# Mish written back into its PSUM bank, and both halves of the result taken from there

## The chip, the core and the metric

One core of a Trainium2 chip runs the whole program, which is launched once. The metric is the device time in microseconds (us): the median over the runs of a kernel. TensorE is called PE in the profile, VectorE DVE, ScalarE ACT and GpSimd POOL.

## The reference

Block-causal attention over four batches of 576 tokens with eight heads of width 64, then an MLP with Mish, then RMS norm and a gated MLP. Only the first MLP is touched by the change.

```
x = attention(q, k, v)                  # 2304 tokens x 512
h = x @ w_in                            # 2304 x 2048
g = h * tanh(log1p(exp(h)))             # Mish
y = g @ w_out                           # 2304 x 512
xn = y / rms(y) * rms_g
out = (silu(xn @ w_gate) * (xn @ w_val)) @ w_out2
```

## The kernel before

**Numbers.** A float32 operand of a product is scaled and split into two float16 halves, "high" and "low" (the rest after the high half). A product is then three passes of float16 matmuls, high by high, high by low and low by high. So each result that goes into another product has to be turned into two halves first: one instruction rounds it to the high half, a second subtracts that from the value and rounds the rest to the low half.

**The first MLP.** Tokens are taken in nine tiles of 256 (t), and d_ff in eight steps (s) of two blocks of 128. A step of `mlp1_h` fills one PSUM bank `ph` (tag `h`, a ring of two banks) with 24 matmuls of 128x256, in two groups of 12: 128 partitions by 512 float32. Then, in every tile but the first, which is computed in float32 and has no halves, three instructions follow:

- line 1410, ACT: Mish of the bank with a scale per partition, written to an SBUF tile `f` (a ring of two),
- line 1419 (DVE), 1422 (ACT) or 524 (POOL): the high half `g[:, 0]`, from `f` with a scale per partition; the three engines are alternatives,
- line 1427, DVE: the low half `g[:, 1]` from `f`, the scale and the high half.

This is done 64 times (eight steps in each of eight tiles). `mlp1_y` then takes `g` (tag `g16`, a ring of four) as the weights of 12 matmuls of 128x512 into two PSUM banks `y`.

**What goes on beside it.** The attention of later tokens is interleaved with it. For each head, PE makes the scores `s` (lines 989, 1000 and 1007, a ring of two banks), DVE takes the row maximum `mx` (1024), DVE or POOL makes a bias of it (1033), ACT makes the exponential `e` (1049), and `e` is split into halves `p`: high by DVE, ACT or POOL (1123, 1126, 524), low by POOL or DVE (1130). A DMA transposes `p` into `pt`, and PE multiplies it with v (1161, `x`). Mish and the exponential need different ACT tables, so ACT loads a table whenever it goes from one to the other (`ACT_TABLE_LOAD` under lines 1049 and 1410). The weights of the second MLP are loaded and split in the same stretch, too.

**The order of the work.** The program records its operations with their reads, writes and alternatives, and a planner (`Plan`) computes from costs and a key of each operation in what order every engine issues, and on which engine an operation with alternatives runs. What comes out is a fixed order for each engine. The keys are shifted by two tables, `SHIFT` (by part of the work) and `FINE` (by number of the operation). A buffer's ring is a wait: the first writer of a buffer waits for all users of the buffer that had its place before. In the second MLP, the accumulators reuse the rings `g16` and `f` (`acc_of`).

Of the kernel before, what the change touches and what calls it, by code (L numbers as in the profile page):

```python
# [334 lines left out]
def block_attention_mish_mlp_gated_mlp(  # L335
# [13 lines left out]
    nc = tc.nc  # L349
# [599 lines left out]
    def attention(b, i, at, pace):  # L949
# [20 lines left out]
        def scores(keys, at):  # L970
# [43 lines left out]
            es = [buf("at", [P, NTT * P], F32, f"e{b}_{i}_{h}", "e", 3) for h in keys]  # L1014
# [27 lines left out]
            for y, (h, e) in enumerate(zip(keys, es)):  # L1042
                if n % P:
                    op(POOL, 125, lambda e=e: nc.gpsimd.memset(e()[:, n : kt * P], 0.0), w=[(e, "pad")], at=at)
                for z, (c0, w) in enumerate(parts):
                    acc = (ssum, h) if len(parts) == 1 else (sump, 2 * key + z)
                    op(
                        ACT, t_act(w, 2, True, True),
                        lambda y=y, z=z, c0=c0, w=w, acc=acc, e=e, h=h: nc.scalar.activation(  # L1049
                            out=e()[:, c0 : c0 + w], in_=ts[z]()[:, y, :], func=AF.Exp, bias=bias()[:, h : h + 1],  # L1050
                            scale=c_op(), accum_out=acc[0]()[:, acc[1] : acc[1] + 1],
                        ),
                        r=[(ts[z], y), (bias, h)] + c_in, w=[(e, z), acc], at=at, table="exp",
                    )
# [211 lines left out]
        for gi, keys in enumerate(groups):  # L1266
            a = at + pace * gi / len(groups)
            plan.part = f"a{b}_{i}_{(4 if b == 0 else 2) * gi // len(groups)}"
            es = scores(keys, a)
            pv, pt = probs(keys, es, a)  # L1270
# [76 lines left out]
    def mlp1_h(t, s):  # L1347
# [49 lines left out]
        if whole:  # L1397
            if n < G_START:
                g32 = plan.part_of(spares, n)
            else:  # L1400
# [7 lines left out]
        e = buf("m1", [P, W], F32, f"f{n}", "f", F_BUFS)  # L1408
        op(
            ACT, t_act(W, 1, True), lambda: nc.scalar.activation(out=e(), in_=phf(), func=AF.Mish, scale=cs()),  # L1410
            r=[ph, (ch[t], q0)], w=[e], at=at, table="mish",
# [4 lines left out]
        hv = lambda: e().rearrange("p (g t) -> p g t", g=SC)  # L1416
        sc = lambda: ich[t]()[:, q0 : q0 + 1]
        op(
            DVE, t_dve2(W, 1), lambda: nc.vector.tensor_scalar_mul(g16()[:, 0], hv(), sc()), r=[e, (ich[t], q0)],
            w=[(g16, 0)], at=at,  # L1420
            alts=[(ACT, t_act(W, 1),
                   lambda: nc.scalar.activation(out=g16()[:, 0], in_=hv(), func=AF.Copy, scale=sc())),  # L1422
                  (POOL, t_pool1(W, 1), lambda: pool_copy(g16()[:, 0], hv(), sc()))],
        )
        op(
            DVE, t_dvett(W, 1),
# [3 lines left out]
            r=[e, (ich[t], q0), (g16, 0)], w=[(g16, 1)], at=at,  # L1430
# [869 lines left out]
```

## Time and profile before

| | |
|---|---|
| median of 3 runs | 951.97 us (951.47 to 953.11) |
| the profiled execution | 951.73 us |
| its span, first to last instruction | 949.9 us |
| granted TensorE clock, mean | 0.999 |
| PE, DVE, ACT, POOL busy | 921.5, 807.5, 657.5, 550.8 us |

The profiled execution lies 0.24 us under the median, and its time is 1.8 us above its span. The stretch of the 64 steps goes from 137 to 560 us. Busy time of PE is the union of the recorded spans of its matmuls; in the first 60 us it has filler matmuls in it, too (`shared<-idle_in`).

### The profile page before, as it was taken

Reading aid. Unit: us, or ns where it says so; the run is one execution under the profiler, and the core shown is the slowest. Engines: PE = TensorE matmul, PEld = TensorE weight load, DVE = VectorE, ACT = ScalarE, POOL = GpSimd, SP = SyncE. Lnnn points to the kernel's source line nnn. Section 1 sums busy time; section 2 is a strip of 40 time slices with the busy share of each in tenths; the row PEclk is TensorE's granted clock in tenths of the full one; section 3 lists DMA queues with packets and bytes.
Section 4 is the critical chain, followed back from the end, with each engine's and each line's share of the span. In section 5 each row is a group of like instructions: output and inputs, shape, how many; then the busy total and the mean of one; then the engine's idle time right before and its main releaser. Section 6 shows DMA issues by size and latency. Waiting matters only on the chain. (4 is left out here: it accounts for less than half of the span.)

```text
span 949.9 us, 20061 instructions
## 1 busy us (share of the span) xinstructions
PE 921.5 (97%) x7241; PEld 632.4 (67%) x7241; DVE 807.5 (85%) x1837; ACT 657.5 (69%) x1369; POOL 550.8 (58%) x688
## 2 busy tenths in 40 slices
PE   9999999998999999999999999999999999999997
PEld 7785457566577757757576745767676666767675
DVE  5899988997886777889877978989999999997666
ACT  4659679999799878889786546657665665553541
POOL 2348245774474654577754839568857697562322
PEclk9999999999999999999999999999999999999999
DMA  9764596779877796778985557826384560708011
GB/s 231 220 198 127 180 179 124 128 133 181 142 132 133 115 167 112 166 129 179 185 174 87 114 167 136 176 58 131 91 180 78 129 128 24 128 8 164 14 67 68
DMA packets 317187, 125.45 MB, mean 132 GB/s; under 512 B 296352, under 2 KB 296352, under 8 KB 317088
## 3 DMA queue, kind: packets, MB, share of 16 engines
q1 hardware_dynamic: 317088, 124.17, 62.4%
q8 instruction: 57, 0.93, 0.4%
q14 instruction: 42, 0.34, 0.1%
HBM read 50.07 MB, written 12.98 MB: 66 GB/s over the span
## 5 line engine op out<-in xcount | busy, mean ns | idle before, releaser
L1384 PE MATMUL h<-x,w1i 128*128 128x256 f16 x1536 | 180.2, 273 | 1.5 <-ACT f L1410 0.8
L1445 PE MATMUL y<-w1o,g 128*128 128x512 f16 x768 | 177.5, 379 | 2.2 <-DVE g L1427 1.1
L1384 PEld LDWEIGHTS <-w1i 128*128 128x128 f16 x1536 | 146.9, 98 | 24.0 <-issue 1.6
L1989 PE MATMUL o<-w2o,pp 128*128 128x256 f16 x1134 | 138.6, 273 | 2.2 <-DVE pp L1899 1.2
L1989 PEld LDWEIGHTS <-pp 128*128 128x128 f16 x1134 | 110.5, 98 | 26.3 <-issue 3.2
L1445 PEld LDWEIGHTS <-g 128*128 128x128 f16 x768 | 71.2, 98 | 79.7 <-issue 2.2
L1830 PEld LDWEIGHTS <-w2g 128*128 128x128 f16 x756 | 73.8, 98 | 47.9 <-issue 3.2
L1830 PEld LDWEIGHTS <-w2v 128*128 128x128 f16 x756 | 73.9, 98 | 44.9 <-issue 0.9
L1024 DVE TENSOR_REDUCE mx<-s 128x1 f32<-128x512 f32 (+4 forms) x128 | 70.3, 556 | 22.3 <-PE s L990 19.8
L1049 ACT ACTIVATE e<-s,bias,cS 128x512 f32<-128x512 f32 (+4 forms) x120 | 72.5, 607 | 14.3 <-POOL bias L1033 6.2
L1830 PE MATMUL v_u<-xnT,w2v 128*128 128x384 f16 x432 | 81.5, 326 | 0.3 <-DVE wc L659 0.2
L1830 PE MATMUL g_u<-xnT,w2g 128*128 128x384 f16 x432 | 78.9, 326 | 0.3
L1130 POOL TENSOR_TENSOR p<-e,p 128x384 f16<-128x384 f32 (+4 forms) x61 | 58.5, 960 | 18.2 <-DVE p L1123 6.8
L1427 DVE SCALAR_TENSOR_TENSOR g<-f,ich,g 128x512 f16<-128x512 f32 x64 | 57.9, 910 | 8.9 <-ACT g L1422 6.3
L1161 PEld LDWEIGHTS <-pt 128*128 128x128 f16 x1128 | 48.1, 98 | 22.6 <-DMA pt<-p 8.4
L1830 PE MATMUL v<-xnT,w2v 128*128 128x384 f16 x324 | 61.5, 326 | 0.0
L1830 PE MATMUL g<-xnT,w2g 128*128 128x384 f16 x324 | 61.1, 326 | 0.2
L1161 PE MATMUL x<-v,pt 128*128 128x64 f16 (+1 forms) x1128 | 55.0, 199 | 4.8 <-DMA pt<-p 4.7
L1049 ACT ACT_TABLE_LOAD x39 | 50.0, 1283 | 3.5 <-DVE bias L1033 2.9
L1410 ACT ACT_TABLE_LOAD x39 | 50.0, 1283 | 1.7 <-DVE g L1427 0.9
L1410 ACT ACTIVATE f<-h,ch 128x512 f32<-128x512 f32 x64 | 43.4, 685 | 8.0 <-PE h L1384 5.1
L1130 DVE TENSOR_TENSOR p<-e,p 128x512 f16<-128x512 f32 (+4 forms) x51 | 39.3, 773 | 4.1 <-ACT p L1126 2.5
(343 smaller groups left out, 2121.8 us busy)
## 6 DMA issues: line engine op xcount, KB each, us to landing
wir<-in_moe_w_in_dram SPq DMA_DIRECT2D x16, 512.0 KB, 5.5
wor<-in_moe_w_out_dram SPq DMA_DIRECT2D x16, 512.0 KB, 4.2
w2rg<-in_moe_w_gate_dram SPq DMA_DIRECT2D x24, 256.0 KB, 3.2
w2rv<-in_moe_w_val_dram SPq DMA_DIRECT2D x24, 256.0 KB, 3.5
w2ro<-in_moe_w_out_dram SPq DMA_DIRECT2D x24, 256.0 KB, 2.7
q<-in_q_dram SPq DMA_DIRECT2D x16, 256.0 KB, 3.9
k<-in_k_dram SPq DMA_DIRECT2D x16, 256.0 KB, 3.9
v<-in_v_dram SPq DMA_DIRECT2D x15, 256.0 KB, 4.0
```

The lines of the kernel that those rows point to most:

```text
L1024: lambda z=z, cols=cols: nc.vector.reduce_max(out=mx()[:, cols], in_=ts[z](), axis=AX.X),
L1049: lambda y=y, z=z, c0=c0, w=w, acc=acc, e=e, h=h: nc.scalar.activation(out=e()[:, c0 : c0 + w], in_=ts[z]()[:, y, :], func=AF.Exp, bias=bi ...
L1130: lo = lambda eng, z=z, ev=ev: eng.tensor_tensor(out=view(p16)[:, z, :, 1, :], in0=ev(0, kt), in1=view(p16)[:, z, :, 0, :], op=ALU.subtract)
L1161: nc.tensor.matmul(xt()[:, cols, :], pv(z)[:, t, ph, :], v16[b, t]()[:, vh, key * w : key * w + w], start=(t == 0 and y == 0), stop=(t == ...
L1384: nc.tensor.matmul(ph()[:, g, :], w1i[fq]()[:, cc, wh, f * P : (f + 1) * P], x()[:, xh * NCC + cc, :], start=(z == 0), stop=(z == 3 * NCC ...
L1410: ACT, t_act(W, 1, True), lambda: nc.scalar.activation(out=e(), in_=phf(), func=AF.Mish, scale=cs()),
L1427: lambda: nc.vector.scalar_tensor_tensor(out=g16()[:, 1], in0=hv(), scalar=sc(), in1=g16()[:, 0], op0=ALU.mult, op1=ALU.subtract),
L1445: nc.tensor.matmul(yps[t, m](), g16()[:, gh, g, m * P : (m + 1) * P], w1o[f]()[:, wh, :], start=(f == 0 and z == 0), stop=(f == NF1 - 1 an ...
L1830: nc.tensor.matmul(b(), w[wo]()[:, wh, cc, :], x()[:, (2 * xo + xh) * 2 + cc, :], start=(first and i == 0), stop=(i == 5), skip_group_chec ...
L1989: nc.tensor.matmul(b()[:, side, :], pps[r][po]()[:, gh, m * P : (m + 1) * P], w[wo]()[:, wh, r, :], start=(first and i == 0), stop=(i == 5 ...
```

## The change

- Mish (line 1410) is written back into `ph`, in place, not into `f`. The ring `f` is gone (`F_BUFS` 2 to 0).
- The high half is taken from `ph`. Its engine is ACT, with DVE as the alternative; POOL is no alternative any more.
- The low half is taken by DVE from `ph` and the high half. So the bank is in use until the low half is done.
- The ring `g16` has six buffers, not four (`G_BUFS`); the two take the place of the two of `f`, of the same size. The six accumulators that reused `g16` and `f` in the second MLP now reuse the six of `g16`.
- `SHIFT` and `FINE` are replaced by other tables, so the order of the whole program is another, the attention and the second MLP included. The count of the recorded operations is the same.
- The ring of `e` keeps its three buffers and gets a name, `E_BUFS`.

```diff
-        e = buf("m1", [P, W], F32, f"f{n}", "f", F_BUFS)
         op(
-            ACT, t_act(W, 1, True), lambda: nc.scalar.activation(out=e(), in_=phf(), func=AF.Mish, scale=cs()),
-            r=[ph, (ch[t], q0)], w=[e], at=at, table="mish",
+            ACT, t_act(W, 1, True), lambda: nc.scalar.activation(out=phf(), in_=phf(), func=AF.Mish, scale=cs()),
+            r=[ph, (ch[t], q0)], w=[ph], at=at, table="mish",
         )
         table_ops.append(plan.ops[-1])
 
         g16 = buf("m1", [P, 2, SC, T1], F16, f"g{n}", "g16", G_BUFS)
-        hv = lambda: e().rearrange("p (g t) -> p g t", g=SC)
+        hv = lambda: ph()
         sc = lambda: ich[t]()[:, q0 : q0 + 1]
         op(
-            DVE, t_dve2(W, 1), lambda: nc.vector.tensor_scalar_mul(g16()[:, 0], hv(), sc()), r=[e, (ich[t], q0)],
+            ACT, t_act(W, 1, True),
+            lambda: nc.scalar.activation(out=g16()[:, 0], in_=hv(), func=AF.Copy, scale=sc()), r=[ph, (ich[t], q0)],
             w=[(g16, 0)], at=at,
-            alts=[(ACT, t_act(W, 1),
-                   lambda: nc.scalar.activation(out=g16()[:, 0], in_=hv(), func=AF.Copy, scale=sc())),
-                  (POOL, t_pool1(W, 1), lambda: pool_copy(g16()[:, 0], hv(), sc()))],
+            alts=[(DVE, t_dve(W, 1), lambda: nc.vector.tensor_scalar_mul(g16()[:, 0], hv(), sc()))],
         )
         op(
-            DVE, t_dvett(W, 1),
+            DVE, t_dve(W, 1),
             lambda: nc.vector.scalar_tensor_tensor(
                 out=g16()[:, 1], in0=hv(), scalar=sc(), in1=g16()[:, 0], op0=ALU.mult, op1=ALU.subtract
             ),
-            r=[e, (ich[t], q0), (g16, 0)], w=[(g16, 1)], at=at,
+            r=[ph, (ich[t], q0), (g16, 0)], w=[(g16, 1)], at=at,
         )
...
-X_BUFS, F_BUFS, G_START, G_BUFS = 2, 2, 4, 4
+X_BUFS, F_BUFS, G_START, G_BUFS = 2, 0, 4, 6
...
+E_BUFS = 3
```

## Rows read from the trace of the kernel before

**Rows 1.** The page's first part: busy time, share of the span, instructions.

```profile
PE 921.5 (97%) x7241; PEld 632.4 (67%) x7241; DVE 807.5 (85%) x1837; ACT 657.5 (69%) x1369; POOL 550.8 (58%) x688
```

**Rows 2.** Windows: stretch, its length, busy time of each engine (instructions), clock, DMA.

```profile
0.00:137.00 137.00, 132.12 (x931) 91.03 (x932) 114.51 (x279) 93.81 (x237) 57.24 (x81) 1.00 0.70 188
137.00:560.00 423.00, 406.42 (x3620) 279.02 (x3621) 355.12 (x933) 348.42 (x690) 257.12 (x374) 1.00 0.76 145
560.00:950.00 390.00, 382.99 (x2692) 262.38 (x2690) 337.83 (x627) 215.30 (x442) 236.41 (x234) 1.00 0.46 99
```

**Rows 3.** Windows inside the stretch of the 64 steps.

```profile
core 0: us, PE busy (x) PEld busy (x) DVE busy (x) ACT busy (x) POOL busy (x), PEclk, DMA share, GB/s
137.00:160.00 23.00, 21.51 (x210) 17.18 (x211) 20.13 (x61) 19.78 (x39) 11.42 (x19) 1.00 0.71 138
160.00:200.00 40.00, 36.35 (x319) 23.32 (x318) 38.62 (x104) 39.25 (x95) 30.96 (x46) 1.00 0.76 131
200.00:250.00 50.00, 44.91 (x425) 30.12 (x423) 42.41 (x130) 45.93 (x79) 29.09 (x42) 1.00 0.87 157
250.00:300.00 50.00, 48.51 (x443) 34.84 (x440) 40.17 (x96) 43.73 (x96) 29.72 (x47) 1.00 0.84 149
300.00:350.00 50.00, 49.22 (x445) 34.03 (x443) 33.97 (x85) 41.82 (x81) 26.68 (x41) 1.00 0.75 125
350.00:400.00 50.00, 48.99 (x461) 33.43 (x459) 40.56 (x142) 40.16 (x69) 25.00 (x37) 1.00 0.73 140
400.00:450.00 50.00, 47.48 (x466) 34.79 (x464) 44.56 (x107) 44.13 (x98) 37.37 (x64) 1.00 0.83 150
450.00:500.00 50.00, 49.46 (x469) 31.94 (x466) 40.81 (x96) 39.01 (x72) 31.98 (x41) 1.00 0.87 183
500.00:560.00 60.00, 60.00 (x410) 39.36 (x409) 53.88 (x117) 34.61 (x71) 34.89 (x41) 1.00 0.55 127
```

**Rows 4.** Waits of PE from 137 to 560: total us, times, longest.

```profile
PE s L989 <- ACT e L1049: 5.6, 9, 1.4
PE x L1161 <- DMA pt<-p: 4.7, 9, 1.0
...
PE h L1384 <- ACT f L1410: 0.8, 3, 0.4
```

**Rows 5.** Groups by line: shapes, count, busy us, mean ns, idle before.

```profile
L1427 DVE SCALAR_TENSOR_TENSOR g<-f,ich,g 128x512 f16<-128x512 f32 x64 | 57.9, 910 | 8.9 <-ACT g L1422 6.3 <-POOL g L524 2.1
L1410 ACT ACT_TABLE_LOAD x39 | 50.0, 1283 | 1.7 <-DVE g L1427 0.9 <-PE h L1384 0.2
L1410 ACT ACTIVATE f<-h,ch 128x512 f32<-128x512 f32 x64 | 43.4, 685 | 8.0 <-PE h L1384 5.1 <-DVE g L1427 2.3
L524 POOL TENSOR_SCALAR g<-f,ich 128x512 f16<-128x512 f32 x24 | 19.3, 805 | 12.7 <-ACT f L1410 11.0 <-ACT xf L1483 1.0 <-PE y L1445 0.2
L1422 ACT ACTIVATE g<-f,ich 128x512 f16<-128x512 f32 x26 | 18.7, 718 | 4.1 <-PE y L1445 3.6
L1419 DVE TENSOR_SCALAR g<-f,ich 128x512 f16<-128x512 f32 x14 | 9.4, 669 | 4.3 <-ACT f L1410 3.4 <-PE y L1445 0.9
```

**Rows 6.** Single lines or tiles: duration min/median/max in ns, first and last start.

```profile
L1427 DVE SCALAR_TENSOR_TENSOR g<-f,ich,g x64: 732/752/1796, 143.4 to 558.9; 128x512 f16<-128x512 f32 x64
L1499 DVE SCALAR_TENSOR_TENSOR xf<-y,rk,rgb x9: 733/749/751, 137.6 to 540.1; 128x512 f32<-128x512 f32 x9
L1403 ACT ACTIVATE g<-h x4: 580/588/597, 66.5 to 77.6; 128x512 f32<-128x512 f32 x4
L2003 ACT ACTIVATE acc_xh<-o,co x1: 681/681/681, 690.1 to 690.1; 128x512 f32<-128x512 f32 x1
L1130 DVE TENSOR_TENSOR p<-e,p x51: 284/692/3500, 129.7 to 497.1; 128x512 f16<-128x512 f32 x12, 128x640 f16<-128x640 f32 x11, 128x128 f16<-128x128 f32 x11, 128x256 f16<-128x256 f32 x10
```

**Rows 7.** Timeline, three engines, 303 to 322: start, us, engine, what, count, idle before.

```profile
303.40 4.09 PE L1384 MATMUL h<-x,w1i 128*128 128x256 f16 x36
307.53 0.69 ACT L1410 ACTIVATE f<-h,ch 128x512 f32<-128x512 f32 x1 [0.30 <-PE h L1384]
308.39 4.09 PE L1384 MATMUL h<-x,w1i 128*128 128x256 f16 x36
320.61 1.06 DVE L1427 SCALAR_TENSOR_TENSOR g<-f,ich,g 128x512 f16<-128x512 f32 x1
```

More of the change, by code (lines that the diff above doesn't have):

```diff
@@ L1013, in scores @@
             passes = 4 if f32 else 2
-            es = [buf("at", [P, NTT * P], F32, f"e{b}_{i}_{h}", "e", 3) for h in keys]
+            es = [buf("at", [P, NTT * P], F32, f"e{b}_{i}_{h}", "e", E_BUFS) for h in keys]
             for z, (c0, w) in enumerate(parts):
@@ L1049, in scores @@
                         lambda y=y, z=z, c0=c0, w=w, acc=acc, e=e, h=h: nc.scalar.activation(
-                            out=e()[:, c0 : c0 + w], in_=ts[z]()[:, y, :], func=AF.Exp, bias=bias()[:, h : h + 1],
-                            scale=c_op(), accum_out=acc[0]()[:, acc[1] : acc[1] + 1],
+                            out=e()[:, c0 : c0 + w], in_=ts[z]()[:, y, :], func=AF.Exp,
+                            bias=bias()[:, h : h + 1], scale=c_op(), accum_out=acc[0]()[:, acc[1] : acc[1] + 1],
                         ),
@@ L1268, in attention @@
             plan.part = f"a{b}_{i}_{(4 if b == 0 else 2) * gi // len(groups)}"
-            es = scores(keys, a)
-            pv, pt = probs(keys, es, a)
+            pv, pt = probs(keys, scores(keys, a), a)
             for z, key in enumerate(keys):
```

303 rows, old and new, of tables (FINE, SHIFT) are left out of this document.

## The prediction

> **What bounds the kernel now.** I read the page's first part, then the windows, then PE's waits, and last the groups and single durations of the three instructions that are edited. PE is busy 921.5 of 949.9 us [rows 1], so nothing can be won but its idle time: 4.9 us before 137, 16.6 in the stretch of the 64 steps (423.0 less 406.42), 7.0 after it [rows 2]. The edit sits in that stretch. There PE's named waits are for the exponential on ACT (5.6 us) and for the transposed probabilities (4.7); for the bank of h it waits 0.8 us in all [rows 4]. So today the stretch loses time where the attention's chain comes late through ACT, DVE, POOL and the DMA, not at the step that is edited.
>
> The windows show on what that loss hangs [rows 3]. In 160 to 250 and 400 to 450, 140 us, PE idles 3.65 + 5.09 + 2.52 = 11.26 us (8.0%), with ACT and DVE busy (39.25 + 38.62 + 45.93 + 42.41 + 44.13 + 44.56) / 280 = 91% on average. In 250 to 400 and 450 to 500, 200 us, it idles 3.8 us (1.9%) with the two at 80%. From 500 on it idles nothing. I use this as a rough price, an estimate from these rows: about 0.56% of PE idle for each point of mean ACT and DVE load. Over the 423 us, and a load counted over 846 us of two engines, 1 us of ACT or DVE work is then worth 0.28 us of time.
>
> **The change part by part.**
>
> *The low half.* 64 instructions on DVE take 910 ns on average, with 732 the shortest and 1796 the longest [rows 5, 6]. The same kind of instruction with its first input in PSUM, line 1499, same shape, takes 733 to 751 [rows 6]. So the arithmetic costs the same and what goes is the stretching, which only the one with two SBUF inputs shows: 64 x (0.910 - 0.745) = 10.6 us less on DVE. The bounds are 0 (if it is stretched as before) and 10.6; I take the whole, since the row is of the same shape.
>
> *The high half.* Now 26 run on ACT (18.7 us), 14 on DVE (9.4), 24 on POOL (19.3) [rows 5]. After, all 64 are on ACT or DVE, out of PSUM. ACT's copy with a scale out of PSUM took 681 ns [rows 6]; no row shows DVE's, and I bound it by the 500 to 750 ns of its instructions of this shape, near the upper end. At 0.69 us the 64 cost 44.2 us, wherever they run. So ACT and DVE together get 44.2 - 18.7 - 9.4 = 16.1 us more and POOL 19.3 less.
>
> *Mish in place.* 685 ns into SBUF [rows 5]. No row shows ACT writing PSUM. Without a scale operand it takes 588 [rows 6], and the longest ACT row of this width is 718 [rows 5]; I take 685 and bound it by 588 and 718, from -6.2 to +2.1 us over the 64.
>
> *Sum on ACT and DVE:* -10.6 + 16.1 = +5.5 us. By the price above this alone is +1.5 us of time.
>
> *What POOL gets free.* POOL loses 19.3 us of 257.1 in the stretch [rows 2, 5]. The attention's low halves (line 1130) and several high halves run on POOL or DVE by the planner's choice, at 692 ns in the median on DVE [rows 6], so POOL can take back up to 19.3 us. I take 15, with bounds 0 and 19.3.
>
> *What the shared path gets free.* That low half on DVE, 51 times in all, goes from 284 to 3500 ns [rows 6]: DVE instructions between SBUF tiles wait while POOL works. The edit takes 64 + 14 such DVE instructions and 24 of POOL away, some 71 us at their shortest. What the remaining ones win no row gives; 0 and 15 us are my bounds (15 is what the 10.6 of the 64 would be if the rest, about as much again and a half, were relieved alike), and I take 5.
>
> The Trainium skill (SBUF — State Buffer, "Who interferes with whom") says that a DVE instruction with two SBUF inputs contends with a POOL instruction that reads SBUF, and one with at most one SBUF input, outside the two-port modes, does not. The trace agrees in the pair 1796 against 751 ns for the longest of lines 1427 and 1499. By the rule POOL's own waits behind the 64 go too, and the 14 copies of line 1419 lose a fast mode with PSUM as source (VectorE: DVE Perf Modes, "Why PSUM operands drop a tier"); I would then stand nearer to the upper bound of the relief, some 2 us lower in time than without it.
>
> *Total:* 5.5 - 15 - 5 = -14.5 us of ACT and DVE work, x 0.28 = -4.1 us. The bounds: nothing given back, +1.5 us, with the slower Mish +2.1; everything, 5.5 - 19.3 - 15 - 6.2 = -35, so -9.8.
>
> *The rest of the order.* The new tables move everything else as well. What that can give or take is bounded by PE's idle time outside the stretch, 4.9 and 7.0 us [rows 2]; I take 0, and 2 us to either side. The two more buffers of `g` cost nothing and let y come later; the accumulators keep six places of the same size.
>
> So the profiled execution's 951.73 becomes 947.6, and as this execution lies 0.24 us under the median, about the same for the median to within the noise. The own range of this case is 942 to 950.
>
> **The rivals.**
>
> *The bank is held too long (slower).* Before, Mish frees the bank; after, the low half does. The timeline has a case: a step of h ends at 307.5, Mish runs at 307.53, and its low half ends at 321.67; PE begins the step after the next, which needs the same bank, 12 matmuls before the end of the run at 308.39, at about 311.0 [rows 7]. So with the new rule this order would stop PE for 10.7 us, and the low halves must be pulled forward. Done at once, Mish, high half and low half take 0.685 + 0.69 + 0.745 = 2.1 us and some tenths for the hand-overs; a step of h takes 24 matmuls, 2.7 us by the run of 36 in 4.09. So the hold just fits behind the next step, with nothing for a queue on ACT or DVE, and ACT is often in the middle of a table load of 1.28 us [rows 5]. If the bank comes 0.67 us late, one instruction, in one of six steps, that is 11 x 0.67 = 7.4 us, and with nothing gained elsewhere 959. It decides from six such waits on, which eat the forecast's 4.1. For it speaks that only two steps can be open instead of two in banks and two in `f`; against it, that `g` is needed by y much later and that PE has y, s and x to put between. The Trainium skill's line for it (PSUM — Partial Sum Buffer, "Summary: rules for kernel authors") is to evacuate promptly, and by it this rival would be the forecast; the 0.8 us that PE waits for the bank now speaks for room.
>
> *ACT becomes the bound (slower).* If the planner puts all 64 high halves on ACT, it gets 44.2 - 18.7 = 25.5 us more on 348.4, and DVE 20 less. ACT is at 98% in 160 to 200 and 92% in 200 to 250 [rows 3]. About 64 / 423 x 90 = 14 of the 64 fall there, 8 of them new on ACT, 5.5 us; PE's loss would be most of that: 956 to 957. Against it: DVE is the alternative.
>
> *Nothing comes of it.* The waits of [rows 4] are latencies of a chain, and freed POOL time shortens no link: 951 to 953, with +1.5 for the added work cancelling a small relief.
>
> **How the numbers follow.** The forecast, 0.50; nothing comes of it, 0.20; the bank, 0.18; ACT, 0.12. Within 0.2% means 950.1 to 953.9, which is about what a measurement of this kernel can tell from no change. The forecast case lies almost wholly below; the two slower ones above: faster 0.50, same 0.20, slower 0.30. The range that leaves out no more than 2 in 10 goes from 941 (the lower bound of the forecast) to 958.
>
> **What would show it.** Right: line 1427 at 745 ns with a maximum under 800; no g on line 524; POOL under 245 us in the stretch; PE's idle there 12 to 13 us. Wrong: a wait of PE's h for DVE's g of more than 4 us in total (the bank); waits for e or p grown in 160 to 250 with ACT at 95% and more (ACT); PE idle outside the stretch changed by more than 3 us (the order).

## The result

The change made the kernel 0.6% slower: 958.22 us median (954.64 to 960.09, 16 runs) against 951.88 (950.81 to 953.93, 16 runs), ratio 1.0059 [1.0049, 1.0069]. The forecast was 947.6, with a range of 941 to 958.

The profiled execution of the changed kernel (954.64 us, span 952.8) is the fastest of its 16 runs; e15 below has a profile of a slower one. The mean granted clock of these 16 runs was 0.990 to 0.998; that of the kernel before was 0.997 to 1.000 in the 25 runs beside e12.

The windows of the changed kernel, to be laid beside [rows 2] (the last one is three microseconds longer):

```profile
0.00:137.00 137.00, 130.15 (x904) 89.74 (x906) 116.90 (x271) 94.16 (x240) 53.66 (x87) 0.99 0.71 188
137.00:560.00 423.00, 408.44 (x3649) 282.11 (x3646) 346.92 (x957) 335.42 (x660) 225.37 (x361) 1.00 0.73 141
560.00:953.00 393.00, 381.83 (x2685) 261.46 (x2682) 339.87 (x650) 215.45 (x439) 232.56 (x232) 1.00 0.47 101
```

In the stretch of the edit PE idles 14.56 us, 2.0 less than before; the sign for the forecast was 12 to 13. Outside it, it idles 6.85 + 11.17 = 18.0 us, where it was 4.9 + 7.0 = 11.9. So the stretch won a little, and the parts that the edit doesn't touch lost 6.1. That is the last of the signs by which the prediction said it would be wrong.

The groups of the edited lines and two single lines (min/median/max in ns), as in [rows 5] and [rows 6]:

```profile
L1424 DVE SCALAR_TENSOR_TENSOR g<-h,ich,g 128x512 f16<-128x512 f32 x64 | 47.5, 745 | 9.9 <-ACT g L1418 9.2
L1408 ACT ACTIVATE h<-h,ch 128x512 f32<-128x512 f32 x64 | 41.9, 659 | 8.2 <-PE h L1383 7.5
L1420 DVE TENSOR_SCALAR g<-h,ich 128x512 f16<-128x512 f32 x36 | 26.7, 743 | 4.6 <-ACT h L1408 4.4
L1418 ACT ACTIVATE g<-h,ich 128x512 f16<-128x512 f32 x28 | 19.2, 685 | 0.9 <-PE y L1442 0.4
```

```profile
L1424 DVE SCALAR_TENSOR_TENSOR g<-h,ich,g x64: 732/749/752, 148.7 to 554.2; 128x512 f16<-128x512 f32 x64
...
L1130 DVE TENSOR_TENSOR p<-e,p x66: 272/559/1446, 131.5 to 507.2; 128x128 f16<-128x128 f32 x19, 128x640 f16<-128x640 f32 x13, 128x256 f16<-128x256 f32 x13, 128x512 f16<-128x512 f32 x11
```

The edited instructions cost about what was forecast: the low half 745 ns and never over 752 (before up to 1796), no high half on POOL, the high half 743 ns on DVE and 685 on ACT where 690 was taken, Mish a little cheaper. The attention's low half on DVE, which the edit doesn't touch, went from a longest of 3500 to 1446 ns.

PE's waits in the stretch, as in [rows 4]:

```profile
PE x L1161 <- DMA pt<-p: 5.8, 8, 1.5
PE h L1383 <- DVE g L1424: 2.8, 4, 1.0
PE s L989 <- ACT e L1049: 1.7, 4, 0.5
```

The wait for the exponential fell from 5.6 to 1.7; the wait for the bank is there, 2.8 us, under the 4 that I had named as the sign of that rival.

One place where PE loses time is just ahead of the first of the 64 steps. The clock and PE's busy time there, and the timeline of the same place:

```profile
130.00:135.00 5.00, 2.14 (x32) 1.14 (x32) 4.57 (x13) 3.30 (x10) 1.57 (x3) 1.00 0.97 224
135.00:140.00 5.00, 3.81 (x24) 2.20 (x25) 3.92 (x17) 3.26 (x13) 1.03 (x3) 0.66 1.14 196
```

```profile
130.46 1.08 PE L1000 MATMUL s<-kT,qT 64*64 64x512 f32 x4 [1.67 <-ACT e L1049]
...
131.47 0.87 PE L1161 MATMUL x<-v,pt 128*128 128x64 f16 x24
...
132.27 0.33 PE L1000 MATMUL s<-kT,qT 64*64 64x64 f32 x4
...
132.86 0.67 DVE L1024 TENSOR_REDUCE mx<-s 128x1 f32<-128x512 f32 x1
...
133.79 0.20 DVE L1024 TENSOR_REDUCE mx<-s 128x1 f32<-128x64 f32 x1
...
134.03 0.15 DVE L1030 TENSOR_REDUCE mx<-mx 128x1 f32<-128x2 f32 x1
134.22 0.15 DVE L1033 TENSOR_SCALAR bias<-mx 128x1 f32<-128x1 f32 x1
...
134.47 0.69 ACT L1049 ACTIVATE e<-s,bias 128x512 f32<-128x512 f32 x1 [0.15 <-DVE bias L1033]
...
135.30 2.19 PE L1000 MATMUL s<-kT,qT 64*64 64x512 f32 x8 [2.69 <-ACT e L1049]
```

This is the loop of one attention step: scores, row maximum, bias, exponential, and only then is the bank free for new scores. PE's order has nothing else to put there: it is busy 2.14 of 5 us, waits 1.67 and then 2.69 us, and at 135.1 the clock falls to its lower level (1.2 GHz) for 3.4 us. In the kernel before, two groups of four `y` matmuls of the float32 tile lay between such scores (1.96 us at 127.43, 1.98 us at 131.15); in the changed order the last such group starts at 117.56. And behind the scores of 134.07 the kernel before has a run of h before the next scores:

```profile
127.43 1.96 PE L1453 MATMUL y<-wos,g 128*128 128x512 f32 x4
...
131.15 1.98 PE L1453 MATMUL y<-wos,g 128*128 128x512 f32 x4
134.07 1.07 PE L1000 MATMUL s<-kT,qT 64*64 64x512 f32 x4 [0.94 <-ACT e L1049]
...
136.98 4.10 PE L1384 MATMUL h<-x,w1i 128*128 128x256 f16 x36 [0.62 <-DMA x<-x16n]
141.01 1.19 PE L1000 MATMUL s<-kT,qT 64*64 64x512 f32 x8
```

The first step of h that is split starts at 141.2 us, where it started at 137.0.

At the other end, from the 168th matmul of the second MLP's first layer to the end, it takes 356.4 us, before 353.4.

### The profile page after: what moved, and what is told of

The parts are those of the page before. It is cut to its first block, busy times and chain, and to the rows that moved or that the text cites. A ratio compares the mean times of both kernels' runs of the same rounds, so it can differ in the third digit from the quotient of the medians.

```text
span 952.8 us, 20025 instructions
## 1 busy us (share of the span) xinstructions
PE 920.4 (97%) x7234; PEld 633.3 (66%) x7234; DVE 803.7 (84%) x1876; ACT 645.0 (68%) x1338; POOL 511.6 (54%) x680
## 4 chain that ended last, share of the span: by engine, by line
PE 42%; DVE 15%; ACT 6%; POOL 5%; DMA 4%; issue 3%; SPq 0%; ACTq 0%; DVEq 0%; POOLq 0%
PE o L1986 9%; PE y L1442 8%; PE h L1383 6%; PE g_u L1827 5%; PE v_u L1827 5%; PE g L1827 4%; PE v L1827 4%; DMA pt<-p 3%; ACT L1049 1%; ACT L1408 1%; ACT e L1049 1%; DVE mx L1024 1%; POOL pp L1896 1%; DVE pp L1896 1%; PE x L1161 1%
## 5 line engine op out<-in xcount | busy, mean ns | idle before, releaser
L1024 DVE TENSOR_REDUCE mx<-s 128x1 f32<-128x512 f32 (+4 forms) x128 | 69.5, 556 | 15.4 <-PE s L990 14.8
L1049 ACT ACTIVATE e<-s,bias,cS 128x512 f32<-128x512 f32 (+3 forms) x120 | 72.5, 608 | 12.8 <-POOL bias L1033 6.8
L524 POOL TENSOR_SCALAR p<-e 128x128 f16<-128x128 f32 (+2 forms) x53 | 24.5, 466 | 58.9 <-ACT e L1049 42.7
L1424 DVE SCALAR_TENSOR_TENSOR g<-h,ich,g 128x512 f16<-128x512 f32 x64 | 47.5, 745 | 9.9 <-ACT g L1418 9.2
L1130 POOL TENSOR_TENSOR p<-e,p 128x384 f16<-128x384 f32 (+4 forms) x46 | 43.9, 954 | 12.8 <-ACT p L1126 8.9
L1408 ACT ACTIVATE h<-h,ch 128x512 f32<-128x512 f32 x64 | 41.9, 659 | 8.2 <-PE h L1383 7.5
```

The lines of the kernel that those rows point to most:

```text
L524: nc.gpsimd.tensor_scalar(out=out_, in0=in_, scalar1=by, scalar2=1.0, op0=ALU.mult, op1=ALU.mult)
L1024: lambda z=z, cols=cols: nc.vector.reduce_max(out=mx()[:, cols], in_=ts[z](), axis=AX.X),
L1130: lo = lambda eng, z=z, ev=ev: eng.tensor_tensor(out=view(p16)[:, z, :, 1, :], in0=ev(0, kt), in1=view(p16)[:, z, :, 0, :], op=ALU.subtract)
L1408: ACT, t_act(W, 1, True), lambda: nc.scalar.activation(out=phf(), in_=phf(), func=AF.Mish, scale=cs()),
L1424: lambda: nc.vector.scalar_tensor_tensor(out=g16()[:, 1], in0=hv(), scalar=sc(), in1=g16()[:, 0], op0=ALU.mult, op1=ALU.subtract),
```

## The experiments

Line numbers: in the kernels with an order written out, lines lie 25 lower (the low half is L1399, the scores L975, the exponential L1024). The device times:

```
                              us median  (range, runs)            ratio to before [95%]
before, beside these runs     951.7 to 952.3
changed kernel                958.22  (954.64 to 960.09, 16)      1.0059 [1.0049, 1.0069]
e1  opening of before         965.17  (964.38 to 968.07, 4)       1.0132 [1.0117, 1.0148]
e2  ending of before          959.53  (957.82 to 960.90, 5)       1.0072 [1.0060, 1.0085]
e3  both                      967.81  (966.78 to 969.27, 4)       1.0164 [1.0150, 1.0178]
e4  more fillers              960.49  (960.27 to 960.79, 4)       1.0086 [1.0072, 1.0100]
e5  Mish to SBUF again        966.69  (965.38 to 968.85, 4)       1.0158 [1.0145, 1.0171]
e6  edit, rearranged          949.67  (947.27 to 953.89, 12)      0.9976 [0.9963, 0.9989]
e7  before, rearranged        953.89  (952.53 to 956.08, 11)      1.0023 [1.0015, 1.0032]
e8  changed, rearranged       955.21  (953.64 to 956.51, 5)       1.0037 [1.0025, 1.0049]
e9  e6, further               951.43  (949.35 to 954.05, 12)      0.9994 [0.9982, 1.0005]
e10 e6, Mish to SBUF          957.30  (952.85 to 960.46, 8)       1.0050 [1.0031, 1.0069]
e11 before, further           955.65  (954.76 to 956.12, 5)       1.0035 [1.0023, 1.0047]
e12 e6 once more              949.84  (947.47 to 955.74, 12)      0.9981 [0.9963, 0.9998]
e13 opening, seam mended      958.84  (957.09 to 959.07, 6)       1.0062 [1.0048, 1.0077]
e14 both, seams mended        960.97  (958.87 to 963.22, 6)       1.0088 [1.0068, 1.0108]
e15 changed kernel again      957.30  (956.16 to 959.27, 6)       1.0050 [1.0033, 1.0066]
e16 changed, seam control     957.25  (955.46 to 957.85, 6)       1.0044 [1.0029, 1.0059]
e17 edit in before's order    976.44  (974.13 to 978.65, 4)       1.0255 [1.0239, 1.0271]
e18 e17, stretch rearranged   945.17  (942.85 to 946.77, 6)       0.9928 [0.9914, 0.9943]
```

Theory A: the edit is a gain, and the order around it costs more than it gives. Theory B: the edit itself costs, by the bank that is held until the low half is taken.

**A book of PE's time.** To tell the parts apart in kernels whose work is cut differently, I kept a book from the traces: elapsed time less the matmul work in it, where a matmul counts as the packed spacing of its shape (20th percentile from start to start in the kernel before) and a filler counts nothing. The work comes to 867 to 868 us in all kernels. What is left is lost time, up to the first split step of h, from there to the end of the first MLP, and after:

```
us lost           opening   stretch   rest    sum
before               35.5      33.4    13.0    81.9
changed              39.6      28.7    16.6    84.9
changed again, e15   42.8      30.2    16.6    89.6
e4                   42.1      32.3    16.7    91.1
e5                   40.4      42.4    16.5    99.3
e6                   42.7      28.2    10.0    80.9
e6 once more, e12    48.1      26.5     9.4    84.0
e7, without the edit 36.2      31.9    16.2    84.3
e9                   38.7      28.7    13.1    80.4
e11, without it      35.6      36.4    14.2    86.2
e10                  44.6      33.5    10.1    88.2
e13                  38.5      34.6    16.3    89.4
e14                  43.7      35.9    13.5    93.1
e16                  38.5      33.4    16.4    88.3
e17                  34.8      58.8    13.0   106.6
e18                  34.3      27.1    12.7    74.1
```

Two cautions go with it. The same program differs from one execution to the next: the opening of the changed kernel has 39.6 and 42.8, that of e6's order 42.7 and 48.1. And the cut at the first split h puts what an order loses just behind that step into the stretch. Counted to fixed times, the kernel before has lost 31.1 us by 130 us, 38.2 by 160 and 43.3 by 200; the changed kernel 30.1, 40.9 and 43.2, and in e15 31.0, 43.8 and 45.6. So the changed order loses more from 130 to 160 us and makes part of it up by 200, in its first profile all of it. There, opening and stretch together lose no more than before (68.3 against 68.9), and the loss that is left lies in the rest.

**How an order is exchanged.** In all order experiments the planner's search is replaced by a list of start times and engine choices; the rest of the program stays as it is.

```diff
-        key = inherit([o.prio for o in self.ops])
...
+        self.seq, picks, start, end = json.loads(zlib.decompress(base64.b85decode(ORDER)))
+        for i, o in enumerate(self.ops):
+            o.start, o.pick, o.end = start[i], picks[i], end[i]
...
-        for o in sorted(self.ops, key=lambda o: (o.start, o.idx)):
+        for o in (self.ops[i] for i in self.seq):
```

"Rearranged" means that steps were moved on their engines, or to an alternative engine, by a search off the chip over the planner's own costs. Places in an order (105 to 175 us, and so on) are the planner's start times; times read from a trace are the chip's.

**e1 to e3: the kernel before's order at the ends.** The changed kernel's code, with ORDER cut together from the two kernels' orders: before the first split h (e1), after the last (e2), both (e3).

> The changed kernel, with the order and the engines of the kernel before up to the first matmul of h that is split in halves (137 us in the trace of before), and its own order from there on. Theory A: the edited steps gain about 4 us, as their first and last h show (137.0 and 549.4 us before, 141.2 and 549.7 after), and the loss is in the opening, +4.2 us with a granted clock of 0.66 in 135 to 140, and after 560, +2.9; then 950 to 954. Theory B: the loss is inside the stretch of the 64 steps, at the bank of h: then 957 to 958, as the changed kernel.

> The changed kernel with its own order up to the last step of h, and from there on with the order and the engines of the kernel before. Theory A: the 2.9 us lost after 560 come back, 955 to 956. Theory B: 957 to 958, nothing comes back.

> The opening and the ending in the order of the kernel before, the stretch between them in the order of the changed kernel, with the edit. Theory A: 947.5 to 951, below the kernel before, because only the gain in the stretch is left. Theory B: 957 to 958.

e1 and e3 missed, because a seam, the cut where two orders meet, costs by itself. In e1 PE waited 8.4 us in one piece for a step of ACT behind the cut, and the first split h came at 147.3 us. e2 has a seam too (3.8 us), so its median doesn't fall; but from the 168th matmul of the second MLP on it took 353.7 us, like the kernel before (353.4), where the changed kernel, e1 and e4 took 356.3 to 356.5. So the changed order of the ending costs 2.9 us by this measure; the opening stayed open.

**e4: is it the clock?** The kernel puts filler matmuls between PE's steps in its first 60 us; here they go on to 140 us.

```diff
-                if last < FILL:
+                if last < 140000.0:
```

> The changed kernel with filler matmuls in PE's waits not only up to 60 us but up to 140 us; all else stays. The 16 runs of the changed kernel lie from 954.6 to 960.1, and its profiled execution, with the clock at 0.66 in 135 to 140, is the lowest of them. If the median's 3.6 us above that come from PE's clock after the waits at 128 to 141 us, the clock stays up and the runs close in on 952 to 955. If not, the runs stay at 957 to 959.

From 130 to 145 us the clock stayed at 1.00, and the first split h came at 143.5 us all the same, 2.3 us later than in the changed kernel's profile. 1.3 of these came at 23.2 us, where e4's clock was at its lower level for 3.4 us; the rest of the way took 1.0 us longer with the clock up than with it down. So PE waits there for the chain of the scores at either level. The fillers stand in PE's queue themselves, so what the upper level alone would be worth isn't shown. In the stretch h waited 5.8 us for the low half.

**e5: the edit undone, the order kept.** Order and engines are those of the changed kernel, but in 48 of the 64 steps Mish goes to a buffer in SBUF (a ring of two), and both halves are taken from there.

```diff
+        e = buf("at2", [P, 2, 256], F32, f"f{n}", "f", 2) if n < 56 else ph
-            ACT, t_act(W, 1, True), lambda: nc.scalar.activation(out=phf(), in_=phf(), func=AF.Mish, scale=cs()),
-            r=[ph, (ch[t], q0)], w=[ph], at=at, table="mish",
+            ACT, t_act(W, 1, True), lambda: nc.scalar.activation(out=e(), in_=ph(), func=AF.Mish, scale=cs()),
+            r=[ph, (ch[t], q0)], w=[e], at=at, table="mish",
...
-        hv = lambda: ph()
+        hv = lambda: e()
```

> The changed kernel with every engine's order and every choice of engine as they are; only Mish goes to a ring of two SBUF tiles again, and both halves are taken from there, in 48 of the 64 steps (the last 16 stay in PSUM, where the SBUF is taken). Theory A (the edit itself gains, by taking the low halves off the path that DVE shares with POOL): low halves back from 745 ns to 850 to 910, PE's lost time between the first and the last h grows, and the time is 958 to 962. Theory B (the edit loses, by holding the bank): PE's waits of h for DVE (2.8 us in the profile of the changed kernel, 5.8 in that with fillers) vanish, and the time falls to 952 to 956.

8.5 us slower than the changed kernel. The groups show the 48 from SBUF above the 16 from PSUM:

```profile
L1400 DVE SCALAR_TENSOR_TENSOR g<-f,ich,g 128x512 f16<-128x512 f32 x48 | 47.7, 996 | 5.7 <-ACT g L1394 5.3
...
L1400 DVE SCALAR_TENSOR_TENSOR g<-h,ich,g 128x512 f16<-128x512 f32 x16 | 11.9, 746 | 3.1 <-ACT g L1394 3.0
```

The wait for the bank was nearly gone, and the time was worse:

```profile
PE h L1358 <- DVE g L1400: 0.7, 1, 0.7
```

So theory B is not why the changed kernel is slow: in this order the bank costs less than the copy in SBUF.

**e6 to e9, e11, e12: other orders.** e6 has the edit and starts from the kernel before's opening and ending and the changed kernel's stretch, rearranged; e9 rearranges that further. e8 is the changed kernel's own order, rearranged. e7 and e11 are the kernel before without the edit, rearranged as long as e6 and e9. e12 was to be e6 with fillers up to 148 us, but the number that was exchanged does not stand in that kernel (its line reads FILL), so what ran was e6 unchanged: the text of e12 is no test, and the run is a repeat.

> The changed kernel with the edit, but another order: it starts from the opening of the kernel before, the stretch of the changed kernel and the ending of before, and single instructions are moved from there for some minutes of search. Theory A (the order that came with the edit loses, not the edit): 944 to 951. Theory B (the bank): 955 and more, with the waits of h for DVE at 3 us and more.

> The kernel before, without the edit, its order rearranged by the same search for the same time. It is the other arm to the rearranged kernel with the edit. Theory A: the same as that one or up to 4 us slower. Theory B: faster than that one by 4 us and more.

> The changed kernel, the same search from its own order, opening and ending included. Theory A: 948 to 954, between the changed kernel and the one that starts from the ends of before. Theory B: 955 and more.

> The edit, with the fixed order of e6 rearranged further (the same steps, engines still chosen per step; no other line differs). Theory A (the edit is worth having, and what made the changed kernel slow is the order it was given around the stretch): the time stays at or below that of e6, 945 to 950 us, and below the kernel before. Rival (the 949.67 of e6 was the luck of one order, and the edit is worth nothing): as likely above as below the kernel before, 950 to 957.

> The kernel before with its own fixed order rearranged further, as far as e9 was. Theory A: the order of the kernel before has little to give, 950 to 955, and e9 lies 3 to 8 us below it. Rival (any rearranging gives what e6 gave, and the edit nothing): 946 to 950, within 1 us of e9.

> e6 with more idle matmuls between its own from 140 to 148 us, where its TensorE clock was granted at half level from 137.9 to 144.8 us. If the half level costs what its length says (6.9 us at half rate, less what waits for ScalarE anyway): 1 to 3 us below e6, 946 to 949. If the opening is set by ScalarE's steps and not by the clock, as the fillers run on the changed kernel had it: within 1.5 us of e6, or above it.

With the edit: 949.67, 951.43 and, from the changed order, 955.21. Without it: 953.89 and 955.65, both above the kernel before. So this search gives nothing to the kernel without the edit, and e6 is below both kernels. Laid beside each other after the same length of search, the kernel with the edit is 4.2 us ahead twice (e6 against e7, e9 against e11), and in the book its stretch loses 28.2 and 28.7 us against 31.9 and 36.4; the two arms did not start from the same order, though. e9 missed its forecast: a longer search gained nothing, so a microsecond or two between such orders is not foretold by the planner's costs. The repeat (e12) lies 0.2 us from e6, each over 12 runs, so the difference between e6 and the kernel before is no luck of a few runs.

**e10: the edit undone in e6's order.** The edit of e5, in e6. (The text says 48 steps; with its limit on n it was 40, as the counts show.)

```diff
+        e = buf("at2", [P, 2, 256], F32, f"f{n}", "f", 2) if n < 48 else ph
```

> e6's order and engines to the last step, but the Mish of the first 48 of the 64 split steps goes to a buffer in SBUF (ring of 2) and both halves are taken from there; the last 16 stay in the PSUM bank. Theory A (halves from PSUM keep DVE's low half off the port that POOL uses, and that is worth more than the bank held longer costs): 6 to 10 us above e6, 955 to 960, the low half from SBUF at a mean of 950 to 1000 ns against 745, and less matmul time in the stretch from 137 to 560 us. Theory B (the bank held until the low half is taken is what costs): at or under e6, 945 to 950, as the wait of h for the low half goes away.

```profile
L1400 DVE SCALAR_TENSOR_TENSOR g<-f,ich,g 128x512 f16<-128x512 f32 x40 | 33.7, 841 | 4.0 <-ACT g L1394 3.8
...
L1400 DVE SCALAR_TENSOR_TENSOR g<-h,ich,g 128x512 f16<-128x512 f32 x24 | 17.8, 743 | 1.4 <-ACT g L1394 1.1
```

7.6 us slower than e6. Per step that went back to SBUF that is 7.6 / 40 = 0.19 us, in e5 8.5 / 48 = 0.18: two orders, much the same price. But both orders were made for the edit, and the arm without it runs in an order that was not made for it. So this is what undoing the edit costs in such an order; what the edit is worth between two orders that each fit is not shown by it.

**e13 to e16: the seams mended.** e13 is e1 with the steps from 105 to 175 us rearranged until none stands in another's way; e14 is e13 with the kernel before's ending and that seam mended too; e16 rearranges the same stretch in the changed order as a control; e15 is the changed kernel itself.

> The changed kernel with the steps of the kernel before's opening in the kernel before's order (as in e1), then its own order; the seam between the two, from about 105 to 175 us, rearranged until no step stands in the way of another, which e1 lacked. The ending is the changed kernel's. Theory A (the changed order of the opening costs about 4 us, before any edited step runs): 953 to 955.5 us, the granted clock of the whole run back above 0.997, the first split h at about 137 us. Rival (the opening is late for another reason, or what it loses is made up in the stretch): 957 to 960 us.

> e13, and behind the last split h the kernel before's order of steps, with that seam (535 to 600 us) rearranged as well. Theory A (opening about 4 us, ending about 3 us, the edit itself a gain): 949.5 to 953 us, 2 to 4 us under e13, and 353 to 354 us from the 168th matmul of the second layer on. Rival (the ends cost nothing, the edit is what costs): 957 to 960 us.

> The changed kernel itself with its order written out: another look at it. The profiled run of the changed kernel was the fastest of its 16 runs (954.64 against a median of 958.22) with a mean granted clock of 0.997 against a median of 0.994. Theory A: 956 to 960 us, and where its profile falls near the median, the half clock level behind ScalarE's waits in the opening lasts longer than the 3.4 us of the first look. Rival (the 3.6 us between that run and the median lie in the stretch, in waits of h for VectorE's halves): the half level as before, and 3 us more of these waits.

> The changed kernel with its own order, rearranged in the same stretch (105 to 175 us) by as much as e13 was: what the rearranging of that stretch gives by itself. Theory A: 956 to 958.5 us, so that what e13 is below it is the opening's order. Rival (the rearranging is what helps, not the kernel before's opening): within 1 us of e13.

Theory A missed in e13 and e14. The kernel before's opening did not bring back its first split h at 137 us: it came at 140.0, behind a wait of 2.66 us for the exponential at 137.6 and with the half clock from 138.5 to 145.3. In the kernel before, a run of 36 matmuls of h (136.98 us, 4.10 long) stands in PE's queue ahead of the next scores (141.01); in the changed order those scores come first, and nothing covers them. So the loss does not lie in the opening's steps but at the joint, in what stands between the last opening scores and the first h. By the book the kernel before, e17 and e18 (below) lose 6.9 to 7.1 us from 130 to 160 us, the changed kernel 10.8, e16 10.5 and e13 9.9. e13 has the `y` groups back and loses 2.5 us up to 135, as e18 does (2.4), but 4.8 from 135 to 140, where e18 has h ahead of the scores and loses 1.0. e14's ending took 354.6 us from the 168th matmul on (e13 356.1), so the ending's price shows again, though the total doesn't fall. e16 lies where e15 does (957.25 against 957.30), so rearranging that stretch gave nothing by itself.

e15's profile is of a run of 959.15 us, 0.9 above the median of the 16. Its span is 957.4, its first split h comes at 144.2 us, and the half level there lasts twice as long as in the first profile:

```profile
135.00:140.00 5.00, 1.55 (x12) 0.84 (x13) 4.24 (x13) 3.06 (x10) 0.30 (x1) 0.89 1.15 225
140.00:145.00 5.00, 4.20 (x24) 2.24 (x22) 4.28 (x29) 3.23 (x9) 1.89 (x3) 0.50 1.13 191
```

By the book that run lost 7.3 us more than the kernel before in the opening, 3.6 more in the rest, and won 3.2 in the stretch. The longer half level is not what makes it slower than the first profile. Laid beside that one, the same matmuls stand 1.5 us later from 24 us on, behind a half level of 3.4 us that began at 22.9; 2.2 us later at 130, 3.8 at 145, and 2.2 again at 200. Another 2 us come between 350 and 400 and stay to the end.

**e17 and e18: the edit in the kernel before's order.** e17 is the run that was missing: the changed code in the old order. 45 steps had to be drawn forward so that no h stands ahead of the low half that frees its bank; the 24 high halves of POOL went to ACT (20) and DVE (4), which makes 46 and 18 in the trace; the text below has the two engines the other way round. e18 rearranges from 137 to 560 us and leaves opening and ending as in the kernel before.

> The edit in the kernel before's order of steps. 45 steps of the split work (Mish and halves) had to be drawn forward past others on their engines, so that a bank is free before the h that takes it next; the 24 high halves that were POOL's go to VectorE (20) and ScalarE (4); every other step stands where it stood in the kernel before, the opening and the ending to the letter. Theory A (the halves from PSUM are cheaper, and what costs is the changed order of the opening's end and of the second layer): 948 to 953. Theory B (the bank held until the low half is taken is what costs, and only an order made for it hides that): 956 to 970, with waits of h for VectorE's halves of over 8 us in the stretch, and an opening and an ending as in the kernel before.

> e17 with the steps from 137 to 560 us rearranged for the edit; opening and ending stay the kernel before's, step for step. Theory A (the edit is worth some 4 us in the stretch once the order there fits it, and the ends need not change for it): 947 to 950.5 us, first split h at about 137 us, from the 168th matmul of the second layer on 353 to 354 us, clock at 0.998 or above. Rival (the clock falls at the end of the opening in every kernel with the edit, whatever the opening's order, as in e6, e9, e13 and e14): 951 to 956, with a half clock level within 135 to 150 us.

e17 is 24.7 us slower than the kernel before, all of it in the stretch. PE's waits there, and one case on the timeline:

```profile
PE h L1358 <- DVE g L1399: 27.1, 22, 3.7
PE x L1136 <- DMA pt<-p: 3.9, 5, 1.3
```

```profile
436.30 1.28 ACT L1383 ACT_TABLE_LOAD   x1
...
437.60 0.66 ACT L1383 ACTIVATE h<-h,ch 128x512 f32<-128x512 f32 x1
...
438.32 0.74 DVE L1395 TENSOR_SCALAR g<-h,ich 128x512 f16<-128x512 f32 x1
...
438.84 0.66 ACT L1383 ACTIVATE h<-h,ch 128x512 f32<-128x512 f32 x1
...
439.10 0.75 DVE L1399 SCALAR_TENSOR_TENSOR g<-h,ich,g 128x512 f16<-128x512 f32 x1
...
439.90 1.27 PE L1358 MATMUL h<-x,w1i 128*128 128x256 f16 x10 [1.07 <-DVE g L1399]
```

Mish comes behind other steps of ACT and a table load, the halves follow one by one, and PE stops 1.07 us until the low half ends at 439.85. This is the rival of the bank, to the letter, in an order that was not made for it. Much of the chain is ACT's: DVE stood idle 14.7 us before its low halves until ACT's high half was done.

```profile
L1399 DVE SCALAR_TENSOR_TENSOR g<-h,ich,g 128x512 f16<-128x512 f32 x64 | 47.5, 746 | 15.3 <-ACT g L1393 14.7
```

So the 24.7 us hang on where the high halves went and how the 45 steps were drawn forward, too; another way to fit the edit into this order was not tried.

e18 is the fastest kernel of the study: 945.17 us, 0.72% under the kernel before and 13.0 us under the changed kernel, with the same edit. Its windows, its low half, its bank wait, and the joint on PE:

```profile
0.00:137.00 137.00, 132.96 (x942) 91.58 (x943) 115.60 (x281) 93.83 (x237) 57.70 (x83) 1.00 0.72 190
137.00:560.00 423.00, 412.32 (x3648) 282.32 (x3646) 350.92 (x1016) 312.05 (x630) 200.16 (x339) 1.00 0.71 142
```

```profile
L1399 DVE SCALAR_TENSOR_TENSOR g<-h,ich,g 128x512 f16<-128x512 f32 x64 | 47.5, 744 | 4.1 <-ACT g L1393 3.8
```

```profile
PE h L1358 <- DVE g L1399: 1.9, 5, 0.6
```

```profile
126.43 1.96 PE L1425 MATMUL y<-wos,g 128*128 128x512 f32 x4
...
130.14 1.98 PE L1425 MATMUL y<-wos,g 128*128 128x512 f32 x4
133.16 1.08 PE L975 MATMUL s<-kT,qT 64*64 64x512 f32 x4 [1.03 <-ACT e L1024]
...
135.85 4.10 PE L1358 MATMUL h<-x,w1i 128*128 128x256 f16 x36 [0.41 <-DMA x<-x16n]
139.88 1.19 PE L975 MATMUL s<-kT,qT 64*64 64x64 f32 x8
```

The `y` matmuls lie between the scores, h stands ahead of the next ones, the clock is 0.999 in the mean, and the first split h starts at 135.8. From the 168th matmul of the second MLP on it takes 353.1 us. The order is cheap at the ends, and the bank costs 1.9 us.

## Why the prediction was wrong

**The step that failed** is "the rest of the order": "I take 0, and 2 us to either side". It had its own bound, PE's idle time outside the stretch, and that bound was no bound: the idle there was 11.9 us and became 18.0. By the book the changed order loses 4.1 us (first profile) to 7.3 (e15) up to the first split step, or 2.7 to 5.6 counted to 160 us, of which e15's half level at 22.9 us makes 1.5; and 3.6 after the stretch. e2, e18 and e17, with the old ending, give 353.1 to 353.7 us for the last part; e1, e4, e5, e13, e15 and e16, with the changed one, 356.1 to 356.5. Up to the first split step e18, with the old opening, loses 34.3 us, the changed kernel 39.6 and 42.8. That the order is the cause, and not the edit, is shown by the same edit in other orders: 945.2 (e18), 949.7 (e6), 951.4 (e9), 955.2 (e8), 958.2 and 976.4 us (e17). The two do not add up, though: in the kernel before's order, as e17 has it, the edit costs 24.7 us, and in the changed order undoing most of it costs 8.5 (e5). Nor has all of the loss one place. The ending has its 3 us or so in every execution of the changed order; the other 3 that the medians lie apart are not in the first profile, and e15 has some 4 us, of which the half level at 22.9 us and what came between 350 and 400 make most. Why these differ from run to run stays open.

**The terms of the edit.** The low half: forecast 0.745, measured 0.745. The high half: 0.69 us for both engines, measured 0.743 on DVE and 0.685 on ACT, 45.9 us in all against 44.2. Mish in place: 685, measured 659, -1.7 us. These are right to within 2 us in the sum.

**What POOL takes back** was wrong in sign: I took 15 us; POOL has 225 us in the stretch, 32 less than before, so it lost 12 us more than the edit took from it. DVE and ACT still have 21 us less together, where I had 14.5; other work was moved in and out of the windows, so I can't split that further. The price of 0.28 us for each would give -5.9; the book gives -4.7 (first profile) and -3.2 (e15), the window 2.0 of PE's idle. Sign and size of the stretch's term, -4.1, are about right, but it rests on a price that no experiment tested, and what is measured hangs on where the stretch is cut.

**The bank.** The rival was given 0.18 and its price as 11 waits of 0.67 us. In the kernel before's order there are 22 waits, 27.1 us (e17); in orders made for the edit it is 1.8 (e8) to 5.8 (e4). So it decides whether the order may stay, not what the edit costs in the end. [rows 7] had said so: one such case was worth 10.7 us, and I left it at "must be pulled forward" without asking what that does to the rest. The Trainium skill's rule (PSUM — Partial Sum Buffer, "Summary: rules for kernel authors") to evacuate promptly holds in e17; in e18 the bank is held for the whole chain and the kernel is the fastest.

**ACT as the bound** did not come: 36.7 of 40 us and 41.2 of 50 in the two windows that I had named.

**The shared path.** The low half from SBUF is stretched again as soon as it goes back there (996 and 841 ns in the mean, longest 1792 in e5), and steady from PSUM (745). The Trainium skill (SBUF — State Buffer, "Who interferes with whom") says that a DVE instruction with two SBUF inputs contends with a POOL instruction that reads SBUF; the runs agree in these means. The relief of the others, taken as 5 us, can be read for the attention's low half on DVE, shape by shape: at the means of the kernel before, its 66 in the changed kernel would have taken 10.5 us more than they did, or 6.4 without the one of 3500 ns.

**What stays open.** Whether the kernel before, rearranged in the stretch alone with both ends kept, would gain as e18 does, was not tried; e7 and e11 rearranged all of it and gained nothing. So how much of e18's 6.6 us is the edit's and how much the search's is not known. Why a longer search (e9) is no better than a shorter one is open too.

## What to carry to other kernels

An edit that comes with a new order is two changes, and they need not add up. Here each cross of the two was slower than both kernels: the edit in the old order (976.4 us) and the changed order with most of the edit undone (966.7). One cross alone would have given a sign for the edit, and the other the opposite one. So give the code with the edit and the code without it an order of its own each, by the same search, before you believe either sign.

Where an instruction comes to hold a buffer longer, look in the timeline for the steps that must move because of it and ask which stall they covered; here the cover that counted most was a run of h ahead of the scores of an attention loop that leaves PE idle for 2.7 us. And PE's idle time outside the edited stretch bounds what a new order can win there, not what it can lose.

## What was not expected of the hardware

- A wait of PE can leave the lower clock behind. After waits of 1.67 and 2.69 us, with PE busy 2.14 of 5 us, the clock went to its lower level for 3.4 us; in another execution of the same program (e15) it did so for 6.8 us after waits of 1.75 and 2.69 us. Filling such waits kept the clock at 1.00 from 130 to 145 us (e4) and did not make the kernel faster. The edit is not needed for it: e7, without it, has the lower level for 3.4 us at 136.4 us. Nor is a wait always needed: in e15 the clock fell at 22.9 us with PE busy 6.79 of the 6.90 us before. The runs of the changed kernel spread over 5.5 us and those of the kernel before over 3.1; that the clock is why is not shown.
- ACT writes Mish into the PSUM bank it reads in 659 ns, 26 ns less than into SBUF (685); in e5, which has both, it is 656 and 685.
- DVE's scaled copy takes 743 ns out of PSUM, steadily (732 to 751); out of SBUF it took 489 in the median in e5 and 602 in the mean, between 468 and 1497. So PSUM is the steadier source for it and not the faster one; what DVE wins by the edit is the low half (745 against 996 ns in e5).
